# A transformer-like block on one core: the first four tiles of x are only centred, and their scale is applied to two products

## The chip, the core and the metric

The kernel runs on one core of a Trainium2 chip. A core has five instruction streams that run side by side and wait for each other by semaphores: PE (TensorE, matrix products, with PEld for the loading of weights), DVE (VectorE), ACT (ScalarE), POOL (GpSimd) and SP (SyncE, which here only starts DMA transfers). DMA transfers can be started by SP and by ACT. The metric is the device time of one execution in microseconds (us); what is compared is the median over several executions.

## What is computed

`x` has 2048 rows of 448 values (bf16). It is normalised by rows, `xn = (x - mean) / sqrt(var + eps)`, and `xn` feeds two branches; the output is `x + A(xn) + B(xn)`.

```python
def _A_ref(x, wqkv, w_phi, wo):                 # linear attention, 16 heads of 28
    q, k, v = split(x @ wqkv)
    pq, pk = q @ w_phi, k @ w_phi               # by head
    phi_q = concat(softmax(pq), softmax(-pq)); phi_k = concat(softmax(pk), softmax(-pk))
    kv = einsum("bhsf,bhsd->bhfd", phi_k, v); z = phi_k summed over s
    num = phi_q @ kv; den = phi_q @ z + 1e-6
    return (num / den) @ wo

def _B_ref(x, w1, w2, w3, w4):
    h = gelu(layernorm(x) @ w1)
    hs = (four column groups of h, shifted by 1, -1, 2, -2 rows) @ w2
    x1 = x + hs
    return x1 + gelu(layernorm(x1) @ w3) @ w4

xn = layernorm(x)
return x + _A_ref(xn, ...) + _B_ref(xn, ...)
```

## The kernel before, in words

The 2048 rows are 16 tiles of 128 rows. Every tile goes through the same steps, and each engine's stream is written out by hand: the order of the calls in the source is the order on each engine, and a recording layer adds the semaphore waits. There is no planner. Nearly every instruction is issued from a helper, so the profile shows few lines: L188 is a matrix product, L192 a transpose on PE, L196 an ACT activation, L200 any elementwise operation (on DVE or POOL), L203 a transposing DMA and L206 a plain DMA.

**The head.** SP and ACT start the loads of x (`xtok`), of V's weights (`wv`, in two halves, one from each engine) and of W1 (`w1`, the same). For each tile DVE takes row statistics (`ln_stats`: one BATCH_NORM_STATS2 on `xtok`, one BATCH_NORM_AGGREGATE that writes mean and variance to `mv`). POOL makes the scale from the variance (`ln1_scale`: an addition and a power, written to `rs`), and DVE subtracts the mean and multiplies with the scale in one TENSOR_SCALAR (`ln1_apply`), which writes `xn`. PE transposes the tile by four 128x128 products with an identity (`xn_T`), ACT copies the result to `xnT`, and PE multiplies it with `wv` and `w1`. V's products leave PSUM as a copy into `vaug` (by ACT or DVE), W1's through a GELU on ACT into `h_tok`, whose scale `rs[..., 4]` is that of the second layer norm. `octet(g)` does this for four tiles: pairs of V and W1 products in eight PSUM banks, full 128-row products first, 64-row tails after. In octet 0 the transposes of tiles 0 to 3 stand among the first products, those of 4 and 5 after the V products of tiles 2 and 3; the transposes of tiles 6 and 7 open octet 1, in banks 4 and 5, which hold the V products of tiles 2 and 3 until DVE has copied them out. Before the first real product PE runs idle products on a constant (`spin`). Tiles 12 to 15 are transposed by DMA (`xn_Td`).

**The middle.** SP transposes `h_tok` to `hT` by DMA (`h_T`), which the shifted products with `w2` read (`w2_tile`, row tile i needs `hT` of tile i+1 too); their sum with `xn` is x1 (`w2_add`), which takes the place of `xn`. K and Q products of four tiles at a time (`ks`, `qs`) go through two exponentials on ACT; DVE and POOL normalise K (`k_norm`); `kv_tile` sums over all 16 tiles in banks 4 and 5. `g_T` transposes the normalised x1 to `gT` by DMA (two buffers, one for each group of four tiles), `eq_T` the exponentials of Q to `eqT`.

**The last stage.** A list `plan` gives for each of nine stages the bank pairs of W3 products (`chunks`, 14 for each group of four row tiles) and the steps between them: `N` (num_tile) a Q product with kv and its division on DVE and POOL, `O` (o_T) a DMA transpose of the result, `E` (eq_T) the next two transposes of Q, `Ff` (fin_full) the products with `w4` and `wo` that need `O`'s transpose, `St` the store, `W`, `ga` and `sc` what is left of the middle.

The places that the change touches are the list of first loads, `ln1_some` and `octet(0)` in the head, the order of `ks`, `qs`, `k_norm` and `w2_tile` in the middle (K's tiles in the order 0, 4, 8, 12, Q's first four behind K's 4 to 7), and two rows of `plan`.

Of the kernel before, what the change touches and what calls it, by code (L numbers as in the profile page):

```python
# [11 lines left out]
LN_EPS = 1e-5  # L12
# [196 lines left out]
def bass_parallel_sum__linear_kernel_hedgehog__mixer_s_mlp__prompt_kernel(  # L209
# [15 lines left out]
    with es:  # L225
# [35 lines left out]
        gT = new("gT", 2 * KC * 512).rearrange("p (b c s) -> p b c s", b=2, c=KC)  # L261
        eq_r = region("eq", 8 * 2 * 512 * 2)
# [29 lines left out]
        mv2 = new("mv2", NT * 8, F32).rearrange("p (t c) -> p t c", t=NT)  # L292
        rs2 = new("rs2", NT * 8, F32).rearrange("p (t c) -> p t c", t=NT)
# [90 lines left out]
        busy = gT[:, 0, 0, 0:256]  # L384
        R.ew(dve, "memset", busy, 1.0)
# [61 lines left out]

        def ln1_apply(eng, i):
            ln_apply(eng, halves(xn[:, i, :]), lap(xtok[:, i, :]), mv, rs, i, 2)
# [3 lines left out]
        def spin(n, cols):  # L453
            for _ in range(n):
                R.mm(banks[3][:, 0:cols], busy[:, 0:128], busy[:, 0:cols], True, True)
# [11 lines left out]
        def xn_T(i, b):  # L467
            b = banks[b]
            for kc in range(KC):
                R.tr(tview(b)[:, 128 * kc:128 * kc + 128], xn[:, i, 128 * kc:128 * kc + 128], ident[:, :])  # L470
            R.act(xnT[:, :, 128 * i:128 * i + 128], tview(b).rearrange("p (c d) -> p c d", c=KC), ACT.Copy)

        def xn_Td(i):
            R.dma_t(xnT[:, :, 128 * i:128 * i + 128], xn[:, i, :])
# [19 lines left out]
        def v_pair(i, b):  # L494
            def out(eng="ACT"):
                vd = vaug[:, i:i + 2, :].rearrange("p t (h e) -> p t h e", e=HP)[:, :, :, 0:DH]
                vs = two(b)[:, :, 0:D].rearrange("p t (h e) -> p t h e", e=DH)
                if eng == "ACT":
# [5 lines left out]
        def w_pair(i, b):  # L504
            def out(ks=(0, 1)):
                for k in ks:
                    R.act(h_tok[i + k].rearrange("p (m d) -> p m d", m=NM)[:, :, 0:CR],
                          banks[b + k][:, 0:D].rearrange("p (m d) -> p m d", m=NM), ACT.Gelu_apprx_tanh,
                          scale=rs[:, i + k, 4:5])
            return [tok(w1, i, b), tok(w1, i + 1, b + 1)], out  # L510

        def k_pair(i, b):
            def out():
                for s in range(2):
                    R.act(phik[:, i:i + 2, s, :], two(b)[:, :, 0:D], ACT.Exp, scale=1.0 - 2.0 * s)
# [41 lines left out]
        def k_norm(i, eng=pool):  # L557
            for j in (i, i + 1):
                ph = phik[:, j, :, :].rearrange("p s (h e) -> p (s h) e", e=DH)
# [6 lines left out]
        def kv_tile(i):  # L566
            for c in range(NC):
                b = banks[4 + c // 2][:, 224 * (c % 2):224 * (c % 2) + 224].rearrange("p (s f) -> p s f", s=2)
                for j in range(2):
                    R.mm(b[64 * j:64 * j + 64, :, 56 * j:56 * j + 56],  # L570
                         vaug[:, i, 128 * c + 64 * j:128 * c + 64 * j + 64],
                         phik[:, i, :, CR * c + 56 * j:CR * c + 56 * j + 56],
                         i == 0 and c % 2 == 0, i == NT - 1)
# [30 lines left out]
        def w2_add(i, b, stats=True):  # L604
            b = banks[b]
            x1, x = xn[:, i, 0:D], xn[:, i, :]
            x = bass.AP(x.tensor, x.offset, [list(x.ap[0]), [288, 2], [1, 224]])
# [337 lines left out]
```

## Time and profile before

| | before |
|---|---|
| median of 3 runs | 181.69 us (181.62 to 182.08) |
| the profiled execution's own time | 181.43 us |
| its span (first to last instruction) | 179.7 us |
| granted TensorE clock in the rows | 1.000 |
| PE busy | 175.9 us, 98% of the span |
| DVE, POOL, ACT busy | 117.6, 94.6, 80.2 us |
| moved by DMA | 21.04 MB, 117 GB/s |

A timeline row reads: start, length, engine, line, operation, output and input tiles, shapes, how many instructions were merged into the row, and in brackets the idle time of the engine ahead of it with what ended it. PE's rows overlap, since products are pipelined: a row's length holds the drain of the last product. The rows of DMA issues (SPq, ACTq) show how long the issuing engine was occupied; when the data landed stands in the table of DMA issues.

### The profile page before, as it was taken

Reading aid. Unit: us, or ns where it says so; the run is one execution under the profiler, and the core shown is the slowest. Engines: PE = TensorE matmul, PEld = TensorE weight load, DVE = VectorE, ACT = ScalarE, POOL = GpSimd, SP = SyncE. Lnnn points to the kernel's source line nnn. Section 1 sums busy time; section 2 is a strip of 40 time slices with the busy share of each in tenths; the row PEclk is TensorE's granted clock in tenths of the full one; section 3 lists DMA queues with packets and bytes.
Section 4 is the critical chain, followed back from the end, with each engine's and each line's share of the span. In section 5 each row is a group of like instructions: output and inputs, shape, how many; then the busy total and the mean of one; then the engine's idle time right before and its main releaser. Section 6 shows DMA issues by size and latency. Waiting matters only on the chain.

```text
span 179.7 us, 3181 instructions
## 1 busy us (share of the span) xinstructions
PE 175.9 (98%) x1218; PEld 90.5 (50%) x1218; DVE 117.6 (65%) x269; ACT 80.2 (45%) x99; POOL 94.6 (53%) x144
## 2 busy tenths in 40 slices
PE   7999999999999999999999999999999999999994
PEld 5554655454445444654554654553554544635564
DVE  5898679659999999584594296196282352655531
ACT  2378881798999639777105104103206006014000
POOL 7774582067999797002457526037835063151660
PEclk9999999999999999999999999999999999999999
DMA  5998555499465498473245545432554654120231
GB/s 166 338 218 134 102 87 104 89 341 223 89 90 106 98 277 172 91 160 60 58 88 89 89 101 104 110 62 58 113 112 99 82 138 96 43 59 28 55 106 51
DMA packets 59142, 21.04 MB, mean 117 GB/s; under 512 B 50744, under 2 KB 58616, under 8 KB 59128
## 3 DMA queue, kind: packets, MB, share of 16 engines
q1 hardware_dynamic: 55656, 16.56, 45.8%
q10 hardware_dynamic: 3472, 4.29, 8.0%
q8 instruction: 9, 0.15, 0.3%
q14 instruction: 5, 0.04, 0.1%
HBM read 7.08 MB, written 1.84 MB: 50 GB/s over the span
## 4 chain that ended last, share of the span: by engine, by line
PE 95%; DVE 3%; ACT 0%; issue 0%
PE bank L188 93%; PE bank L192 2%; DVE vaug L200 1%; DVE st L200 1%; DVE xn L200 1%; ACT xnT L196 0%; DVE mv L200 0%; DVE gT L200 0%
## 5 line engine op out<-in xcount | busy, mean ns | idle before, releaser
L196 ACT ACTIVATE phik<-bank 128x1024 bf16<-128x1024 f32 (+1 forms) x44 | 40.2, 991 | 68.1 <-PE bank L188 67.9
L188 PE MATMUL bank<-gT,w 128*128 128x512 bf16 (+1 forms) x224 | 46.1, 380 | 0.1
L188 PE MATMUL bank<-w,phik 128*128 128x448 bf16 (+2 forms) x238 | 45.2, 342 | 0.0
L200 DVE TENSOR_TENSOR vaug<-bank,vaug 128x464 f32<-128x464 f32 (+3 forms) x65 | 33.1, 514 | 17.4 <-PE bank L188 12.3
L200 POOL TENSOR_TENSOR xnT<-vaug 128x196 bf16<-128x196 f32 (+1 forms) x32 | 18.0, 585 | 49.2 <-DVE vaug L200 49.2
L188 PEld LDWEIGHTS bank<-w,phik 128*128 128x128 bf16 x238 | 22.6, 98 | 18.4 <-issue 0.2
L188 PEld LDWEIGHTS bank<-gT,w 128*128 128x128 bf16 (+1 forms) x224 | 17.9, 97 | 24.0 <-issue 5.1
L200 POOL TENSOR_TENSOR phik<-phik,rks 128x896 bf16<-128x896 bf16 x15 | 25.8, 1754 | 1.0 <-DVE rks L200 0.9
L200 POOL TENSOR_TENSOR vaug<-xn,xtok 128x448 f32<-128x448 bf16 x16 | 16.3, 1029 | 1.4 <-DVE vaug L200 1.4
L200 DVE TENSOR_TENSOR xn<-bank,xn 128x448 bf16<-128x448 f32 x16 | 9.4, 597 | 11.5 <-PE bank L188 11.5
L200 DVE TENSOR_REDUCE ksum<-phik 128x32 f32<-128x896 bf16 x16 | 16.6, 1035 | 0.0
L200 DVE RECIPROCAL vaug<-bank 128x16 f32<-128x16 f32 x16 | 3.6, 228 | 17.9 <-PE bank L188 17.9
L188 PE MATMUL bank<-wo,xnT 128*128 128x448 bf16 (+3 forms) x68 | 14.7, 344 | 0.0
L200 POOL TENSOR_TENSOR rs<-mv,mhalf 128x2 f32<-128x2 f32 (+1 forms) x16 | 13.8, 863 | 1.3
L188 PE MATMUL bank<-w,hT 112*128 112x448 bf16 x64 | 14.2, 352 | 0.0
L188 PE MATMUL bank<-wv,xnT 128*128 128x448 bf16 (+1 forms) x64 | 14.0, 354 | 0.1
L188 PE MATMUL bank<-w,xnT 128*128 128x448 bf16 (+1 forms) x64 | 13.9, 352 | 0.0
L188 PE MATMUL bank<-wpk,xnT 128*128 128x448 bf16 (+1 forms) x64 | 12.2, 354 | 0.0
L188 PE MATMUL bank<-wpq,xnT 128*128 128x448 bf16 (+1 forms) x64 | 12.1, 354 | 0.0
L196 ACT ACTIVATE eq<-bank 128x896 bf16<-128x896 f32 x12 | 10.0, 923 | 1.4 <-PE bank L188 1.4
L200 POOL TENSOR_SCALAR mv<-mv 128x4 f32<-128x4 f32 x4 | 0.8, 203 | 18.2 <-DVE mv L200 18.2
L200 DVE BATCH_NORM_STATS2 st<-xtok 128x6 f32<-128x448 bf16 x16 | 9.8, 612 | 0.8 <-DMA xtok<-in_A_x_dram 0.7
(66 smaller groups left out, 179.2 us busy)
## 6 DMA issues: line engine op xcount, KB each, us to landing
w<-in_B_w_dram ACTq DMA_DIRECT2D x2, 896.0 KB, 6.4
out_dram<-vaug SPq DMA_DIRECT2D x15, 112.0 KB, 1.9
w<-in_B_w_dram ACTq DMA_DIRECT2D x1, 1568.0 KB, 8.7
xtok<-in_A_x_dram SPq DMA_DIRECT2D x2, 448.0 KB, 6.8
wo<-in_A_wo_dram SPq DMA_DIRECT2D x2, 224.0 KB, 2.8
w<-in_B_w_dram SPq DMA_DIRECT2D x1, 392.0 KB, 4.4
hi<-eq SPq DMA_TRANSPOSE x24, 2.5
xtok<-in_A_x_dram SPq DMA_DIRECT2D x3, 112.0 KB, 3.0
```

The lines of the kernel that those rows point to most:

```text
L188: self.op("PE", lambda e: e.matmul(out, lhsT, rhs, start=start, stop=stop, skip_group_check=True), [out], [lhsT, rhs])
L192: self.op("PE", lambda e: e.transpose(out, in_, ident), [out], [in_, ident])
L196: self.op("ACT", lambda e: e.activation(out, in_, func, **kw), [out], [in_] + aps)
L200: self.op(eng, lambda e: getattr(e, name)(out, *args, **kw), [out], aps)
```

## The change

Tiles 0 to 3 of x are no longer scaled before the transposes. `ln1_center` on DVE subtracts the mean and multiplies with 1.0, right behind the tile's own statistics, into `xc`, which lies in the second buffer of `gT`. PE transposes `xc`. The scale is applied later: to V's products as they leave PSUM (one instruction for each of two tiles, with the scale `rs[..., 2]`, where one copy took both tiles), and to W1's products in the GELU's scale, for which `ln1_first` makes `rw` in three small DVE operations. K, Q and the residual still need the scaled tiles, so POOL makes them later (one TENSOR_SCALAR for four means, four `ln1_apply` into `xc`), and four more DMA transposes on SP write them over the first four tiles of `xnT`. K's order is turned so that tiles 0 to 3 come last (4, 8, 12, 0; `phik`'s slots and `kv_tile`'s sum too), and Q's first four tiles move behind K's 12 to 15.

With it: x's first tile is loaded in two halves of 64 rows, one from SP and one from ACT; both halves of `wv` are started ahead of x's tile 2, x's tile 5 goes to SP; the constant of the idle products is set by POOL as its first instruction, and the idle products are 31 of 128 columns, then 4; the copy of tile 0's transposes is made in two halves; the transposes of tile 5 stand three products later; W1's tiles 0 and 1 leave PSUM together; and in two stages of the plan `O` stands ahead of `E`.

```diff
+        xc = gT[:, 1, :, :]
...
+        rw = new("rw", 4 * 8, F32).rearrange("p (t c) -> p t c", t=4)
...
-        load_x(0, 1)
+        busy = gT[:, 0, 0, 0:128]
+        R.ew("POOL", "memset", busy, 1.0)
+        for k, e in enumerate(("SP", "ACT")):
+            R.dma(xtok[64 * k:64 * k + 64, 0, :], x2d[64 * k:64 * k + 64, :], e)
         load_x(1, 1, "ACT")
+        load_lap(wv, A_wqkv[:, 896:1344], ("ACT", "SP"))
         load_x(2, 1)
-        load_lap(wv, A_wqkv[:, 896:1344], ("ACT", "SP"))
         load_x(3, 1, "ACT")
+        load_lap(w1, B_w1, ("ACT", "SP"))
         load_x(4, 1)
-        load_lap(w1, B_w1, ("ACT", "SP"))
-        load_x(5, 1, "ACT")
+        load_x(5, 1)
...
+        def ln1_first():
+            R.ew(dve, "scalar_tensor_tensor", rw[:, :, 0], rs[:, 0:4, 3], (1.0 + LN_EPS) ** -0.5, mv[:, 0:4, 2],
+                 op0=ALU.mult, op1=ALU.mult)
+            for k in range(2):
+                R.ew(dve, "tensor_tensor", rw[:, :, 1 + k], rw[:, :, k], rs[:, 0:4, 2], op=ALU.mult)
...
+        def ln1_center(i):
+            R.ew(dve, "tensor_scalar", halves(xc[:, i, :]), lap(xtok[:, i, :]), mv[:, i, 0:1], 1.0, op0=ALU.subtract,
+                 op1=ALU.mult)
...
+            for c in (slice(0, 4, 3), slice(1, 3)) if i < 1 else (slice(0, 4),):
+                R.act(xnT[:, c, 128 * i:128 * i + 128], tview(b).rearrange("p (c d) -> p c d", c=KC)[:, c, :], ACT.Copy)
...
+                if i < 4:
+                    for k in range(2):
+                        s = rs[:, i + k, 2:3]
+                        if eng == "ACT":
+                            R.act(vd[:, k, :, :], vs[:, k, :, :], ACT.Copy, scale=s)
+                        else:
+                            R.ew(eng, "tensor_scalar", vd[:, k, :, :], vs[:, k, :, :], s, 1.0, op0=ALU.mult, op1=ALU.mult)
...
-                          scale=rs[:, i + k, 4:5])
+                          scale=rs[:, i + k, 4:5] if i > 3 else rw[:, i + k, 2:3])
...
-        def ln1_some(a, n):
-            for i in range(a, a + n):
-                ln1_stats(i, 1, 0)
-                if i:
-                    ln1_apply(dve, i - 1)
-                if i == 4:
-                    ln1_again(0, 4)
+        def ln1_some():
+            for i in range(4):
+                ln_stats(st, mv, xtok, i)
+                ln1_center(i)
+                if i % 2:
+                    ln1_scale(i - 1, 2, 0)
+            ln1_stats(4, 1, 0)
+            ln1_stats(5, 1, 0)
+            ln_stats(st, mv, xtok, 6)
+            ln1_apply(dve, 4)
+            ln_stats(st, mv, xtok, 7)
+            ln1_scale(6, 2, 0)
+            ln1_apply(dve, 5)
+            ln1_first()
...
-                spin(19, 256)
-                xn_T(0, 4)
-                spin(5, 128)
-                xn_T(1, 5)
+                spin(31)
+                xn_T(0, 4, xc)
+                spin(4)
+                xn_T(1, 5, xc)
...
+        R.ew(pool, "tensor_scalar", rs[:, 0:4, 1], mv[:, 0:4, 0], -1.0, 0.0, op0=ALU.mult, op1=ALU.add)
+        for i in range(4):
+            ln1_apply(pool, i)
...
+        h_T(5)
+        for i in range(4):
+            xn_Td(i)
+        for i in range(6, 8):
...
-        ks(0)
+        ks(4)
...
-        batch([nxt(k_pair, 4)], [nxt(k_pair, 6)], folds)
+        batch([nxt(k_pair, 8)], [nxt(k_pair, 10)], folds)
...
-            (0, 2, 6, [(Ff, 6), (St, 4), (N, 8, 0), (E, 12), (O, 8), (N, 9, 6), (E, 13), (O, 9), (Ff, 7), (St, 5),]),
+            (0, 2, 6, [(Ff, 6), (St, 4), (N, 8, 0), (O, 8), (E, 12), (N, 9, 6), (O, 9), (E, 13), (Ff, 7), (St, 5),]),
```

What stands in a row now, at the places where instructions move. First DVE at the start of the program, from its first statistics on (`st` and `mv` hold them, `xtok` is x as loaded, `rs` the scale). Before:

```order
L200 BN_STATS st<-xtok 128x6
L200 BN_AGGR mv<-st 128x2
L200 BN_STATS st<-xtok 128x6
L200 BN_AGGR mv<-st 128x2
L200 TENSOR_SCALAR xn<-xtok,mv,rs 128x512
```

After:

```order
L200 BN_STATS st<-xtok 128x6
L200 BN_AGGR mv<-st 128x2
L200 TENSOR_SCALAR gT<-xtok,mv 128x512
L200 BN_STATS st<-xtok 128x6
L200 BN_AGGR mv<-st 128x2
```

The first tile is centred directly behind its own statistics, and the operation reads no `rs`, so POOL is no longer between them.

DVE again, up to the V products of tiles 2 and 3 that it takes out of banks 4 and 5. Before:

```order
L200 BN_STATS st<-xtok 128x6
L200 BN_AGGR mv<-st 128x2
L200 TENSOR_SCALAR xn<-xtok,mv,rs 128x512
L200 CAST vaug<-bank 128x32x28
L200 BN_STATS st<-xtok 128x6
```

After:

```order
L200 TENSOR_SCALAR xn<-xtok,mv,rs 128x512
L200 SCALAR_TENSOR_TENSOR rw<-rs,mv 128x4
L200 TENSOR_TENSOR rw<-rw,rs 128x4 x2
L200 BN_STATS st<-xtok 128x6
L200 BN_AGGR mv<-st 128x2
L200 TENSOR_SCALAR xn<-xtok,mv,rs 128x512 x2
L200 TENSOR_SCALAR vaug<-bank,rs 128x16x28 x2
```

One copy of both tiles became two scaled ones, and the last two tiles of x stand directly ahead of them.

SP's first loads. Before:

```order
L206 DMA xtok<-in_A_x_dram 128x448 x2
L206 DMA wv<-in_A_wqkv_dram 128x2x448
L206 DMA xtok<-in_A_x_dram 128x448
L206 DMA w<-in_B_w_dram 128x2x448
L206 DMA xtok<-in_A_x_dram 128x2x448
```

After:

```order
L206 DMA xtok<-in_A_x_dram 64x448
L206 DMA wv<-in_A_wqkv_dram 128x2x448
L206 DMA xtok<-in_A_x_dram 128x448
L206 DMA w<-in_B_w_dram 128x2x448
L206 DMA xtok<-in_A_x_dram 128x448 x2
L206 DMA xtok<-in_A_x_dram 128x2x448
```

x's tile 2 was SP's second load and is its third, behind a half of `wv`.

SP's transposes in the middle (`hT` from three tiles of `h_tok`, called hi, w and h here; `hi<-eq` are those of Q). Before:

```order
L203 DMA_TRANSPOSE xnT<-xn 128x4x128 x4
L203 DMA_TRANSPOSE hi<-in_A_wqkv_dram 128x448 x2
L203 DMA_TRANSPOSE hT<-hi 128x4x128 x3
L203 DMA_TRANSPOSE hT<-w 128x4x128 x3
L203 DMA_TRANSPOSE gT<-g_tok 128x4x128 x4
L203 DMA_TRANSPOSE hi<-eq 128x4x128 x8
```

After:

```order
L203 DMA_TRANSPOSE xnT<-xn 128x4x128 x4
L203 DMA_TRANSPOSE hi<-in_A_wqkv_dram 128x448 x2
L203 DMA_TRANSPOSE hT<-hi 128x4x128
L203 DMA_TRANSPOSE xnT<-gT 128x4x128 x4
L203 DMA_TRANSPOSE hT<-hi 128x4x128 x2
L203 DMA_TRANSPOSE hT<-w 128x4x128 x3
L203 DMA_TRANSPOSE gT<-g_tok 128x4x128 x4
L203 DMA_TRANSPOSE hT<-w 128x4x128
L203 DMA_TRANSPOSE hi<-eq 128x4x128 x8
```

Four transposes are new, and all that stands behind them on SP moves back by four places, the second group of `gT` too.

More of the change, by code (lines that the diff above doesn't have):

```diff
@@ L514, in out @@
                 for s in range(2):
-                    R.act(phik[:, i:i + 2, s, :], two(b)[:, :, 0:D], ACT.Exp, scale=1.0 - 2.0 * s)
+                    R.act(phik[:, (i + 12) % 16:(i + 12) % 16 + 2, s, :], two(b)[:, :, 0:D], ACT.Exp, scale=1.0 - 2.0 * s)
             return [tok(wpk, i, b), tok(wpk, i + 1, b + 1)], out
@@ L571, in kv_tile @@
                          vaug[:, i, 128 * c + 64 * j:128 * c + 64 * j + 64],
[L572 to L573 removed]
+                         phik[:, (i + 12) % 16, :, CR * c + 56 * j:CR * c + 56 * j + 56],
+                         i == 4 and c % 2 == 0, i == 3)
         def kv_copy():
@@ L744, in octet @@
                 xn_T(i + 4, 0)
-                xn_T(i + 5, 1)
+                if g:
+                    xn_T(i + 5, 1)
             if late:
                 late()
-            w[1]((1,))
+            w[1]((1,) if g else (0, 1))
             v2[1](evac)
-            for o in w2[0]:
+            for k, o in enumerate(w2[0]):
                 full(o, False)
+                if not g and not k:
+                    xn_T(5, 1)
             w2[1]()
-        ln1_some(0, 8)
+        ln1_some()
         ln_stats(st, mv, xtok, 8)
-        ln1_apply(dve, 7)
+        for i in range(6, 8):
+            ln1_apply(dve, i)
         octet(0, "DVE")
@@ L776, in bass_parallel_sum__linear_kernel_hedgehog__mixer_s_mlp__prompt_kernel @@
             load_wT(0, c)
-        for i in range(5, 8):
+        h_T(5)
+        for i in range(4):
+            xn_Td(i)
+        for i in range(6, 8):
             h_T(i)
```

65 lines of the change are left out of this document (33 added, 32 removed).

## The prediction

> **What bounds the kernel now.** I read the busy times first, then the chain that ended last, then the timeline of the first 16 us.
>
> ```profile
> PE 175.9 (98%) x1218; PEld 90.5 (50%) x1218; DVE 117.6 (65%) x269; ACT 80.2 (45%) x99; POOL 94.6 (53%) x144
> ```
>
> ```profile
> 1.26 4.24 PE bank L188 x19
> ...
> 21.79 54.50 PE bank L188 x430
> ```
>
> The chain is PE nearly throughout, and in the 54.50 us of 430 products nothing but PE stands. So a change pays only where PE idles or runs idle products: ahead of the first real transposes at 5.46, between them, and in single stalls. The work behind the head cannot get shorter; it can only start earlier or be held up anew.
>
> ```profile
> 3.07 0.59 DVE L200 BATCH_NORM_STATS2 st<-xtok 128x6 f32<-128x448 bf16 x1 [0.75 <-DMA xtok<-in_A_x_dram]
> ...
> 4.99 0.41 DVE L200 TENSOR_SCALAR xn<-xtok,mv,rs 128x512 bf16<-128x512 bf16 x1 [0.38 <-POOL rs L200]
> ...
> 5.46 0.61 PE L192 MATMUL bank<-ident,xn 128*128 128x128 bf16 x4
> ...
> 6.46 0.63 DVE L200 BATCH_NORM_STATS2 st<-xtok 128x6 f32<-128x448 bf16 x1
> ...
> 8.30 0.39 PE L192 MATMUL bank<-ident,xn 128*128 128x128 bf16 x4
> ...
> 8.53 0.73 PE L188 MATMUL bank<-w,xnT 128*128 128x448 bf16 x3
> ...
> 10.03 0.62 DVE L200 BATCH_NORM_STATS2 st<-xtok 128x6 f32<-128x448 bf16 x1
> 10.69 0.18 DVE L200 BATCH_NORM_AGGREGATE mv<-st 128x2 f32<-128x6 f32 x1
> 10.98 0.41 DVE L200 TENSOR_SCALAR xn<-xtok,mv,rs 128x512 bf16<-128x512 bf16 x1
> 11.31 0.62 DVE L200 BATCH_NORM_STATS2 st<-xtok 128x6 f32<-128x448 bf16 x1
> ...
> 12.06 0.38 DVE L200 TENSOR_SCALAR xn<-xtok,mv,rs 128x512 bf16<-128x512 bf16 x1
> ...
> 13.63 1.08 DVE L200 CAST vaug<-bank 128x896 bf16<-128x896 f32 x1
> ...
> 14.77 0.45 PEld L192 LDWEIGHTS bank<-ident,xn 128*128 128x128 bf16 x8 [0.34 <-DVE vaug L200]
> ...
> 15.23 0.73 PE L188 MATMUL bank<-wv,xnT 128*128 128x448 bf16 x3
> ```
>
> DVE works nearly without a break from 3.07 to 14.71. The last place in the head where PE waits for it is the eight transposes of tiles 6 and 7, which need banks 4 and 5 copied out; behind them PE goes on at 15.23. I call this the gate: whatever moves the gate moves the end.
>
> **The change part by part.** The pace at the gate has two possible owners, DVE and the loads.
>
> *DVE.* Before, from tile 3's statistics (6.46) to the copy's end (14.71) are 8.25 us. A tile's TENSOR_SCALAR starts 0.75 behind the statistics ahead of it (11.31 to 12.06), or 0.95 where it waits for POOL (10.03 to 10.98). After, the stretch holds one TENSOR_SCALAR fewer (the centring is done behind the own statistics): -0.33, the step from 10.98 to the next operation at 11.31. Waits for POOL go: two of 0.2 and one of 0.1 at tile 2, -0.48. One small operation more than before: +0.20. Centring waits for its own aggregate, start at 0.87 (10.03 to 10.69, 0.18 and 0.03) instead of 0.75: +0.12. The copy becomes two:
>
> ```profile
> 27.29 1.14 DVE L200 CAST wpk<-bank 128x448 bf16<-128x448 f32 x2
> ```
>
> Wait-free, two copies of this size take 1.14 against 1.08: +0.06 (between 0 and 0.15). Sum 8.25 - 0.33 - 0.48 + 0.20 + 0.12 + 0.06 = 7.82. Ahead of it stands tile 2's statistics and centring, 1.18 (0.87 and 0.31). With 0.06 to start, and 0.28 from the copy's end through the second tile's transposes, PE passes the gate at L + 9.34, if DVE's tile 2 starts at L, the landing of x's tile 2. It passed at 15.23, so L = 5.89 breaks even. Without any wait for loads DVE starts tile 2 at about 5.1 (first statistics some 0.3 sooner for the halved load, an estimate, at 2.75; two tiles of 1.18).
>
> *The loads.* Landing is issue time and the time in the table of DMA issues.
>
> ```profile
> xtok<-in_A_x_dram SPq DMA_DIRECT2D x3, 112.0 KB, 3.0
> xtok<-in_A_x_dram ACTq DMA_DIRECT2D x3, 112.0 KB, 4.7
> wv<-in_A_wqkv_dram ACTq DMA_DIRECT2D x1, 224.0 KB, 4.1
> wv<-in_A_wqkv_dram SPq DMA_DIRECT2D x1, 224.0 KB, 5.2
> w<-in_B_w_dram ACTq DMA_DIRECT2D x1, 224.0 KB, 5.4
> ```
>
> ```profile
> 1.26 0.46 ACTq L206 DMA_DIRECT2D wv<-in_A_wqkv_dram  x1
> 1.72 0.43 SPq L206 DMA_DIRECT2D wv<-in_A_wqkv_dram  x1
> 1.75 0.49 ACTq L206 DMA_DIRECT2D xtok<-in_A_x_dram  x1
> 2.27 0.46 ACTq L206 DMA_DIRECT2D w<-in_B_w_dram  x1
> ```
>
> So `wv`'s ACT half landed at 5.4 as the queue's 336th KB, x's tile 3 at 6.45 and `wv`'s SP half at 6.9 (both 448), W1's ACT half at 7.7 (672). Tile 2 moves from SP's second place (started beside `wv`'s ACT half at about 1.26, landed 3.0 later, 4.3) to the third, with 392 KB on its queue. Its bounds are 4.3 and 6.9; the middle of the two ACT rows is 5.9, and a tile of x lands 0.45 sooner than a weight half with as many bytes (6.45 against 6.9). I take L = 5.45: the gate at 14.79, 0.44 sooner. W1's ACT half moves to 728 KB, at the slope of the last two rows (1.25 us for 224 KB) 8.0. From W1's first product to the gate PE needs 15.23 - 8.53 - 0.06 (its stall there) = 6.64: 14.70, so DVE decides. The idle products take 0.223 each for 256 columns (4.24 / 19); 31 of half that from about 1.1 on end at 4.5, so real transposes start there, 1.0 sooner. The halved first load, the sooner idle products and the halved copy gain nothing of their own, since the loads cover them; leaving POOL out starts the first TENSOR_SCALAR 1.05 sooner (3.07 + 0.87 against 4.99), and of that 0.44 reaches the gate.
>
> The Trainium skill (DMA: Bandwidth & Descriptors, "Issuing engines are not separate DMA queues") says that transfers from all issuing engines run on the same 16 DMA engines and interleave. By that, halving saves only issue time, and tile 2 lands with all the bytes ahead on both queues, at the unshifted middle of 5.9; the sum would have nothing at the gate instead of 0.44. The rows of equal bytes with different landings say it is not bytes alone.
>
> *SP and POOL.* Four transposes more:
>
> ```profile
> 24.45 5.13 SPq L203 DMA_TRANSPOSE xnT<-xn  x4
> ...
> 37.28 5.52 SPq L203 DMA_TRANSPOSE hT<-w  x3
> ...
> 71.14 5.13 SPq L203 DMA_TRANSPOSE gT<-g_tok  x4
> ```
>
> ```profile
> SPq L203 <- DVE g_tok L200: 5.9, 1, 5.9
> ```
>
> ```profile
> 78.51 5.78 PE L188 MATMUL bank<-gT,w 128*128 128x512 bf16 x29
> ```
>
> They cost 5.1 on SP, which is busy from 24 to 66 us, so everything behind them comes 5.1 later, until SP's wait of 5.9 for DVE ahead of `gT`'s second group takes it up. During a large weight load a transpose holds SP for 1.84 (5.52 / 3) instead of 1.28; two to four more fall into that, 1.1 to 2.2. So the group starts 0.3 to 1.4 later (5.1 + 1.1 - 5.9, and so on). Its last transpose, issued at 75.0, landed at 77.5 (the landing time is in the next rows), and now by 78.9. PE needs it six products into 78.51, at 79.8. Between 0 and 0.3 (one more transpose held for 1.3); I take 0. K's 12 to 15 now stand ahead of tile 5's W2 product, which so starts behind one batch of 2.9 from 42.6 on, at 45.5, and needs at its second product (45.7) the transpose of `h_tok`'s tile 6. That one takes the place of the third in the row at 37.28 (issued at 40.0):
>
> ```profile
> gT<-g_tok SPq DMA_TRANSPOSE x16, 2.5
> ...
> hT<-w SPq DMA_TRANSPOSE x4, 5.6
> ```
>
> ```profile
> 42.61 3.02 PE L188 MATMUL bank<-wpq,xnT 128*128 128x448 bf16 x16
> ```
>
> It lands (second row; the first is for the group above) at 45.6: between 0 and 0.3, taken as 0. POOL's four new TENSOR_SCALARs take 0.41 on DVE (10.98); even at three times that, an estimate of 5 us, they fit POOL's longest idle stretch, which follows them:
>
> ```profile
> 37.13 0.20 POOL L200 TENSOR_SCALAR mv<-mv 128x4 f32<-128x4 f32 x1 [9.10 <-DVE mv L200]
> ```
>
> They cost nothing; without that cover they would delay K's normalisation by those 5. The turned order of K and Q keeps counts and the turns of the banks:
>
> ```profile
> 54.35 3.35 ACT L196 ACTIVATE phik<-bank 128x896 bf16<-128x896 f32 x4 [0.28 <-PE bank L188]
> ```
>
> ACT waited for PE here, so it is not behind. Its last four exponentials now follow a batch with no W2 tile behind it and end up to 0.75 later against the first W3 products; between 0 and 0.7, taken as 0, since the first bank pair is free one pair of exponentials sooner.
>
> *O ahead of E.*
>
> ```profile
> 133.97 2.50 SPq L203 DMA_TRANSPOSE hi<-eq  x2
> 136.52 1.26 SPq L203 DMA_TRANSPOSE xnT<-xnT  x1
> ...
> 140.84 0.30 PEld L188 LDWEIGHTS bank<-wo,xnT 128*128 128x128 bf16 x3 [0.39 <-DMA xnT<-xnT]
> ```
>
> In one of the two stages PE waits for this transpose; of the 0.39 a weight load hides 0.27, leaving 0.12. Issued 2.5 sooner it is there: -0.12. The other stage has no such stall.
>
> **Sum.** -0.44 - 0.12 = -0.56 against the profiled execution's 181.43 (span 179.7 and 1.73 around it): 180.9. The median of the runs lies 0.26 above it; the forecast for the median is 181.1.
>
> **Rivals.**
> (a) Loads are no bound: tile 2 by 5.1 and W1 by 7.6 at the latest. The gate at 14.4, 0.85 sooner, with 0.12: 180.7. For it: before, x's tile 2 landed well ahead of its use. Against: landings up to 5.4 us behind the issue.
> (b) Nothing comes of the centring, because tile 2 waits for all bytes ahead (L = 5.9): only -0.12 remains, 181.6. For it: the two ACT rows with 336 and 448 KB. [...]
> (c) Slower: SP's third load lands like SP's third load before, `wv`'s half, at 6.9. The gate at 16.3, 1.05 later; less 0.12: 182.6. It decides from L = 6.6 on. For it: same queue, same place, similar bytes. Against: half its size.
> (d) The second group of `gT` lands 1.7 later than I reckon, for transposes held longer by W4's load: a stall of 0.8 at 79.8, 181.9.
> The Trainium skill (TensorE: Matmul & The Clock Gate, "What's actually happening") has the array at half rate until a free-running window of about 3.4 us was busy; the trace agrees that early transposes take longer (0.61 at 5.46, 0.39 at 8.30). If the window fell one turn later, real products to 10 us would run at half rate, an estimate of 1 us; I give it 0.02, within slower.
>
> **How the numbers follow.** The bound of same is 0.3%, 0.55 us, about what a measurement here can tell from no change. Forecast 0.40 (180.8 to 181.4, two thirds of it over the bound), (a) 0.18, (b) 0.17, (c) 0.16, (d) and late clock 0.09. Faster 0.27 + 0.18 = 0.45; same 0.13 + 0.15 = 0.28; slower 0.27. The forecast's own range is 180.8 to 181.4; the range to hold 8 in 10 reaches from beyond (a), 180.4, into (c), 182.3.
>
> **What would show it.** Right: DVE's first TENSOR_SCALAR at 3.7 to 4.0 with no wait for POOL, real transposes at 4.5, the gate passed near 14.8, no stall at `gT`'s second group and none at `wo`'s products in the stage at 140. Wrong: a wait of DVE for `xtok` at tile 2 that reaches past 5.9, PE idle ahead of W1's first product past 8.5, or a new PE wait for a DMA near 45 or 80.

## The result, and the profile after

The changed kernel takes 182.86 us (median of six, 182.73 to 183.21), the kernel before 181.78 us in the same comparison (181.59 to 182.08): a ratio of 1.006, 95% interval 1.0046 to 1.0074. The forecast was 181.1 (180.8 to 181.4; the range to hold 8 in 10 ended at 182.3); the change costs 1.08 us, and the measured time lies beyond both. The profiled execution took 182.73 us with a span of 181.0, against 181.43 and 179.7: 1.30 more.

The first line of the changed kernel's page gives the busy times; the rows below it are from its chain of waits (start, length, what).

```profile
PE 174.0 (96%) x1220; PEld 90.4 (50%) x1229; DVE 117.1 (65%) x270; ACT 80.7 (45%) x101; POOL 96.0 (53%) x144
```

```profile
0.82 0.57 ACTq L206
1.42 0.85 ACTq L206
2.31 0.46 ACTq L206
2.79 4.55 DMA xtok<-in_A_x_dram
7.37 0.64 DVE st L200
...
10.22 0.71 POOL rs L200
10.96 0.41 DVE xn L200
...
28.95 4.16 DMA xnT<-xn
33.11 0.14 issue
33.25 25.57 PE bank L188 x179
```

Before, the chain was PE nearly throughout. Now it runs through three issues on ACT and the landing of x's tile 3 into DVE's list (DVE waited for it only 0.04), and past the gate once more through a DMA: a transpose of one of tiles 12 to 15, 4.16 us long. The head as the timeline shows it (DVE's rows, then PE's):

```profile
3.39 0.63 DVE L200 BATCH_NORM_STATS2 st<-xtok 128x6 f32<-128x448 bf16 x1 [0.23 <-DMA xtok<-in_A_x_dram]
...
4.27 0.35 DVE L200 TENSOR_SCALAR gT<-xtok,mv 128x512 bf16<-128x512 bf16 x1
4.96 0.63 DVE L200 BATCH_NORM_STATS2 st<-xtok 128x6 f32<-128x448 bf16 x1 [0.33 <-DMA xtok<-in_A_x_dram]
...
6.10 0.62 DVE L200 BATCH_NORM_STATS2 st<-xtok 128x6 f32<-128x448 bf16 x1
...
7.37 0.63 DVE L200 BATCH_NORM_STATS2 st<-xtok 128x6 f32<-128x448 bf16 x1
...
10.63 0.18 DVE L200 BATCH_NORM_AGGREGATE mv<-st 128x2 f32<-128x6 f32 x1
10.96 0.41 DVE L200 TENSOR_SCALAR xn<-xtok,mv,rs 128x512 bf16<-128x512 bf16 x1
...
14.26 1.27 DVE L200 TENSOR_SCALAR vaug<-bank,rs 128x448 bf16<-128x448 f32 x2
```

```profile
4.68 0.40 PE L192 MATMUL bank<-ident,gT 128*128 128x128 bf16 x4 [0.36 <-DVE gT L200]
...
6.24 0.40 PE L192 MATMUL bank<-ident,gT 128*128 128x128 bf16 x4 [0.94 <-DVE gT L200]
...
8.90 0.74 PE L188 MATMUL bank<-w,xnT 128*128 128x448 bf16 x3 [0.61 <-DMA w<-in_B_w_dram]
...
15.09 0.89 PE L192 MATMUL bank<-ident,xn 128*128 128x128 bf16 x8
15.82 0.73 PE L188 MATMUL bank<-wv,xnT 128*128 128x448 bf16 x3
```

Centring does start sooner (4.27 against 4.99), and so do the real transposes (4.68 against 5.46). But DVE waits for tile 1 until 4.96; tile 2, landed at 5.11, follows without a break only at 6.10, and tile 3 at 7.37. Before, tiles 1 and 2 were taken up at these times, and tile 3 at 6.46:

```profile
3.79 0.60 DVE L200 BATCH_NORM_STATS2 st<-xtok 128x6 f32<-128x448 bf16 x1
...
5.32 0.62 DVE L200 BATCH_NORM_STATS2 st<-xtok 128x6 f32<-128x448 bf16 x1
```

Tile 1 had landed at 3.18 before and lands at 4.93 now; tile 3 at 6.43 and now at 7.35. W1's first product waits until 8.90 (8.53 before), and the gate is passed at 15.82, not 15.23.

The second loss stands at 32.4. PE's timeline there, and the table of DMA between 29.8 and 31.0 (of the issues in it the one that PE waits for, with its time to landing):

```profile
32.41 0.35 PE L188 MATMUL bank<-wv,xnT 64*128 64x448 bf16 x1
33.25 0.35 PE L188 MATMUL bank<-wv,xnT 64*128 64x448 bf16 x1 [0.49 <-DMA xnT<-xn]
```

```profile
q8 instruction: 1, 0.02, 7.9%
issues: line engine op xcount, KB each, median us to landing
xnT<-xn SPq DMA_TRANSPOSE x1, 4.2
```

The transpose issued at 28.95 landed 4.2 us later, at 33.1; its like before took 2.5 (28.31 to 30.83, one microsecond ahead of its use). While it was under way one packet of 16 KB of the kind "instruction" came through queue q8, at 30.15. Before, that packet came at 31.92, behind the landing.

The starts of PE's products, compared stage by stage, give the whole difference: +0.59 at the gate, +0.83 between the gate and K's first product (the wait at 32.4), 0.00 from there to 140, -0.13 at 140. Sum +1.29 of the 1.30. Rival (d)'s stall didn't happen in this execution: the last transpose of `gT`'s second group landed at 79.90 (77.50 before). The first product that needs it is the seventh of its row, as before at 79.8; with PE 1.42 later it stands at about 81.2, so 1.3 us were to spare (2.3 before), less than the packet at 32 cost its transpose. Another packet of q8 came at 79.91, just behind the landing.

### The profile page after: what moved, and what is told of

Read it like the earlier page. It is cut to its first block, busy times and chain, and to the rows that moved or that the text cites. A ratio compares the mean times of both kernels' runs of the same rounds, so it can differ in the third digit from the quotient of the medians.

```text
span 181.0 us, 3211 instructions
## 1 busy us (share of the span) xinstructions
PE 174.0 (96%) x1220; PEld 90.4 (50%) x1229; DVE 117.1 (65%) x270; ACT 80.7 (45%) x101; POOL 96.0 (53%) x144
## 4 chain that ended last, share of the span: by engine, by line
PE 73%; DVE 12%; DMA 5%; POOL 4%; issue 2%; ACT 2%; ACTq 1%
PE bank L188 73%; DVE st L200 4%; DVE vaug L200 3%; POOL rs L200 3%; DMA xtok<-in_A_x_dram 3%; DVE xn L200 2%; DMA xnT<-xn 2%; ACT phik L196 2%; DVE mv L200 1%; ACTq L206 1%; POOL mv L200 1%; DVE wpk L200 1%; POOL xn L200 0%; DVE rs L200 0%; PE bank L192 0%
## 5 line engine op out<-in xcount | busy, mean ns | idle before, releaser
L188 PE MATMUL bank<-gT,w 128*128 128x512 bf16 (+1 forms) x215 | 44.1, 379 | 0.9 <-DVE vaug L200 0.3
L200 DVE TENSOR_TENSOR vaug<-bank,vaug 128x464 f32<-128x464 f32 (+3 forms) x65 | 33.1, 514 | 17.4 <-PE bank L188 13.5
L200 DVE TENSOR_TENSOR xn<-bank,xn 128x448 bf16<-128x448 f32 x12 | 7.1, 590 | 10.7 <-PE bank L188 10.7
L200 POOL TENSOR_TENSOR rs<-mv,mhalf 128x4 f32<-128x4 f32 (+1 forms) x13 | 12.7, 974 | 1.0
L200 DVE BATCH_NORM_STATS2 st<-xn 128x6 f32<-128x448 bf16 x16 | 9.9, 619 | 0.4
```

The source lines that it names most:

```text
L188: self.op("PE", lambda e: e.matmul(out, lhsT, rhs, start=start, stop=stop, skip_group_check=True), [out], [lhsT, rhs])
L200: self.op(eng, lambda e: getattr(e, name)(out, *args, **kw), [out], aps)
```

## Experiments

For every run its gate and its later waits were read in the same way from its profiled execution. The kernel before, run beside each set, had medians of 181.78 to 181.80. In all fourteen profiles that one's time is 166.2 us behind its gate, plus its later waits, less 0.13 where the wait at 140 is missing, to within 0.15 us. Several kernels spread by up to 2.65 us over their executions (one by more, as said there); where the text names a wait it is that of the profiled one.

**What moves the wait at 32.** If q8's packet does it, its place should follow PE's count of products, of which eleven idle ones more stand ahead. The first kernel takes the changed kernel back to 24 idle products, with narrower products to fill the time:

```diff
-                spin(31)
+                spin(20, 192)
...
-                spin(4)
+                spin(4, 128)
```

> The changed kernel with 24 idle products, as before, in place of 35 (20 of 192 columns and 4 of 128 in place of 31 and 4 of 128; the time they cover stays within 0.2 us). Theory (instruction fetch): the 0.83 us that PE waits at 32.4 for the transposes of tiles 12 to 15 comes from a 16 KB packet of the instruction queue q8, which came at 31.92 in the kernel before and at 30.15 now, because it follows PE's count of instructions and eleven idle products more stand ahead of it. With 24 the packet comes at about 32 to 32.6 again, behind the transposes' landing, and the stall goes: 182.86 - 0.83 = 182.0 (181.9 to 182.2), with the gate still near 15.8. Rival (SP late): the stall comes from SP, whose transposes start 0.65 later, and from the four more transposes; the count of idle products then changes nothing: 182.9 (182.7 to 183.0).

Measured: 183.59 us (181.79 to 184.44), ratio 1.0072 (1.004 to 1.0105). The packet came at 32.57, the fourth transpose landed in 2.5 us, and the wait at 32 was gone; the three quickest executions (181.79, 181.96, 181.99) are at the forecast of 182.0. The profiled one took 183.86, for two other reasons:

```profile
6.59 2.45 PE L188 MATMUL bank<-wv,xnT 128*128 128x448 bf16 x6
...
9.26 1.22 PE L188 MATMUL bank<-w,xnT 128*128 128x448 bf16 x3
```

Six V products took 2.45 us where they take 1.59 in the changed kernel, three of W1 1.22 against 0.74: PE ran at half pace until 10, and the gate came at 16.38. This is the late clock that the prediction gave 0.02. The Trainium skill (TensorE: Matmul & The Clock Gate, "What's actually happening") has the window of the gate free-running, so that the same kernel can turn fast at different places. The same idle products with the old loads, below, were followed by full pace from 5.78 on (four transposes in 0.40, here 0.61 at 6.19); that agrees, but PE had no pause of 0.50 there as it has here ahead of 6.19, and no run shows the window itself. The other loss, 1.38 at 80.7, is rival (d), with a q8 packet at 79.83.

The next kernel takes the idle products of the kernel before (19 of 256 columns and 5 of 128), which keep PE busy longer:

```diff
-                spin(31)
+                spin(19, 256)
...
-                spin(4)
+                spin(5, 128)
```

> The changed kernel with the idle products of the kernel before (19 of 256 columns and 5 of 128), all else as changed. The first run with 24 idle products lost the wait near 32 but had two new losses in its profiled execution: products at half pace up to 10.0, and a wait of 1.38 at 80.7 for the last transpose of gT's second group, which a q8 packet at 79.8 held up. Theory (three separate places): the longer idle products keep the pace, so the gate is near 15.8; the q8 packet comes at about 32 and the wait near 32 is gone: 182.0 in executions in which gT's second group lands in time, up to 1.4 more in those in which a packet meets it; median 182.0 to 182.8. Rival (SP late): the wait near 32 is back, 182.8 to 183.0 in all executions.

Measured: 182.26 us (181.71 to 184.16), ratio 1.004 (1.0007 to 1.0073); six of twelve executions lie between 181.71 and 182.07. Full pace from the first V product, packet at 32.80, no wait at 32. The profiled execution (184.11) is one of the late ones. Its PE row behind 80, and the DMA between 79.0 and 80.4:

```profile
82.60 0.59 PE L188 MATMUL bank<-gT,w 128*128 128x512 bf16 x2 [1.78 <-DMA gT<-g_tok]
```

```profile
q8 instruction: 1, 0.02, 5.9%
issues: line engine op xcount, KB each, median us to landing
gT<-g_tok SPq DMA_TRANSPOSE x1, 3.6
```

The third transpose of the group, issued at 77.51, landed only at 81.92, the fourth at 82.40; a loss of 1.94. Not all of it is this packet's: the fourth was issued at 78.81, so that at the usual 2.5 it would have landed at 81.3, and PE needed it at 80.7. So the changed kernel has two places at which a q8 packet can meet a transpose with little slack, 32 and 80: the three profiles with 35 idle products lost at 32, and of the three with 24 and all of the change's transposes two lost at 80.

The other direction, 50 idle products:

```diff
-                spin(31)
+                spin(46, 88)
```

> The changed kernel with 50 idle products in place of 35 (46 of 88 columns and 4 of 128, which take about the same time). Theory (instruction packet): the second packet of q8 moves another fifteen products forward, from 30.15 to 27 to 28.5, and meets the second or third of the four transposes instead of the fourth; that one lands up to 1.7 later, at 31 to 31.9, still ahead of the 32.4 at which PE needs it, so the wait near 32 goes or falls below 0.3: 182.0 to 182.3, unless a later packet meets gT's second group (1.4 to 1.9 more). Rival: the wait does not hang on the packet's place: 182.8 to 183.0.

Measured: 182.53 us (181.94 to 183.59), ratio 1.0035 (1.0016 to 1.0054); four executions between 181.94 and 182.04, the profiled one among them; what the others lost is not shown. The packet came at 28.27 and met the second transpose, which landed 4.7 us behind its issue where its like before took 2.5; PE waited 0.23 ahead of its product at 30.73 and not at 32. The changed kernel's wait therefore hangs on the packet's place.

Last, the kernel before with 35 idle products, in the same time:

```diff
-                spin(19, 256)
+                spin(30, 160)
```

> The kernel before with 35 idle products in place of 24 (30 of 160 columns and 5 of 128 in place of 19 of 256 and 5 of 128; their time stays 4.2 us), nothing else. Theory (instruction fetch): the packet of q8 comes some eleven products sooner, at about 29.8 to 30.2 in place of 31.92, while the transposes of tiles 12 to 15 are in flight (issued 24.45 to 28.31, last landing 30.83, needed at 31.8), and the first one at about 14.4 in place of 16.42: a wait of 0.4 to 0.9 near 32, 182.2 to 182.7. Rival (SP late): without SP's later start nothing is lost, since there was 1.0 us of slack: 181.8 (181.6 to 181.9).

Measured: 182.06 us (181.48 to 182.86), ratio 1.0012 (0.9995 to 1.003): nothing decided. The packet moved less than expected, to 31.61, and the last transpose had landed at 31.36, 0.25 us ahead of it. In all fourteen traces this packet came when PE had begun 208 to 218 products (the next one at 328 to 336); that scatter of ten products is nearly 2 us, so eleven idle products more make a meeting likely, not sure.

**What moves the gate.** The changed kernel with the first loads of the kernel before, then the same with 24 idle products as above:

```diff
-        for k, e in enumerate(("SP", "ACT")):
-            R.dma(xtok[64 * k:64 * k + 64, 0, :], x2d[64 * k:64 * k + 64, :], e)
+        load_x(0, 1)
         load_x(1, 1, "ACT")
+        load_x(2, 1)
         load_lap(wv, A_wqkv[:, 896:1344], ("ACT", "SP"))
-        load_x(2, 1)
...
```

> The changed kernel with the first loads of the kernel before (x's first tile whole, the old order and the old engines), all else as changed. Theory (loads): the gate at 15.82 is late because x's tile 3 lands at 7.35 and W1's second half at 8.86, against 6.43 and 8.24 before. With the old loads DVE starts tile 3 at about 6.6 and ends the copy 8.16 later (as measured now), at 14.8, W1's first product starts at 8.3 to 8.5 and PE passes the gate at 15.0 to 15.2: 0.6 to 0.8 sooner. The wait near 32 stays: 182.1 to 182.3. Rival (DVE): the gate is late because centring, two small copies and the three operations for rw make DVE's list longer, whatever lands when: gate at 15.6 to 15.8, 182.7 to 182.9.

> Both edits at once: old loads and 24 idle products in the changed kernel. If both theories hold and the two losses are separate, 182.86 - 0.83 - 0.7 = 181.3 (181.1 to 181.6), which is faster than the kernel before by 0.4: the centring's own gain (gate 15.0 to 15.2 against 15.23) and 0.1 for the order of o and q. If the loads are no cause, 182.0; if the idle products are none, 182.1; if neither, 182.9.

Measured: 182.86 us (182.56 to 183.61), ratio 1.0064 (1.0043 to 1.0084), and 182.12 us (181.14 to 183.64), ratio 1.0032 (1.0001 to 1.0064). In the first, tile 3 landed at 7.22 even with the old loads, the gate came at 15.69, and the wait at 32 took 1.08: in time it was no better than the changed kernel, against the expectation. DVE's list there was no longer than in the changed kernel (8.16) and DVE stood idle for tile 3 for 0.47, so a load was late again, though issued at 1.75 as in the kernel before. The five profiles with the old loads have tile 1 landing at 3.18 to 3.50 and tile 3 at 6.18 to 7.22; the six with the new ones 4.75 to 5.07 and 7.02 to 7.44. Tile 1 is late in each of them, tile 3 by 0.6 in the mean. In the second's profiled execution (181.29) tile 3 landed at 6.67, the gate came at 15.22, and no later wait stood anywhere. Its four quickest executions (181.14 to 181.29) lie below the quickest of the kernel before beside it (181.40); the slowest take 2.5 us more.

The reverse tells more: the kernel before with the new loads alone, that is with the same lines the other way round.

> The kernel before with the changed kernel's first loads alone (x's first tile in halves from SP and ACT, wv ahead of x's tile 2, tile 5 on SP). Theory (loads): x's tile 3 lands at about 7.3 and W1's last half at 8.6 to 8.9, in place of 6.4 to 6.9 and 8.2; the gate, which stood 8.8 behind tile 3's landing in the two profiles of the old kernel, comes at 15.9 to 16.2 in place of 15.2 to 15.7: 182.2 to 182.6 against 181.8. Rival (DVE): the gate is late for the centring's own operations and the loads have slack: 181.7 to 181.9.

Measured: 182.76 us (182.09 to 183.63, and one execution of twelve at 186.28), ratio 1.005 (1.0028 to 1.0072). In the median the loads alone cost about what the whole change costs. The profiled execution (182.09), one of the two quickest, has the gate at 16.03, 0.80 later, and no other loss; what the slower ones lost in addition is not shown. DVE's rows for tiles 1 and 3:

```profile
4.84 0.63 DVE L200 BATCH_NORM_STATS2 st<-xtok 128x6 f32<-128x448 bf16 x1 [0.64 <-DMA xtok<-in_A_x_dram]
...
7.18 0.62 DVE L200 BATCH_NORM_STATS2 st<-xtok 128x6 f32<-128x448 bf16 x1
```

DVE waits 0.64 for tile 1 and not at all for tile 3, which comes later only because tile 1 did.

Which part of the loads? The changed kernel with tile 0 whole on SP, all else as changed:

```diff
-        for k, e in enumerate(("SP", "ACT")):
-            R.dma(xtok[64 * k:64 * k + 64, 0, :], x2d[64 * k:64 * k + 64, :], e)
+        load_x(0, 1)
```

> The changed kernel with x's first tile loaded whole by SP; the order of the other loads stays as changed (wv ahead of tile 2, tile 5 on SP). Theory (a place in ACT's list): the half tile on ACT pushes tile 1, wv, tile 3 and W1 one place back; without it tile 1 lands at 3.2 to 3.6 in place of 4.9, tile 3 at 6.4 to 7.2 in place of 7.35, W1's ACT half at 7.7 to 8.4 in place of 8.86; the gate comes at 15.1 to 15.7 in place of 15.82 and the wait near 32 stays: 182.2 to 182.7. Rival (the order): what delays tile 3 and W1 is wv's halves ahead of them, not the half tile; the gate stays at 15.8: 182.8 to 183.0.

Measured: 182.58 us (182.20 to 184.24), ratio 1.0042 (1.002 to 1.0064), gate at 15.47, tile 1 landed at 3.57, tile 3 at 6.15, W1's ACT half at 7.51; the wait at 32 stayed (1.03, packet at 30.49). So tiles 1 and 3 and W1 were late for the half tile, not for the order: it takes a place in ACT's list, and issuing is slower with it. Of the 0.59 at the gate 0.24 is left: here DVE began at 3.40 (3.07 before) and waited 0.12 for tile 2, which stands behind `wv` and landed at 5.87, so the order may have a part in that. ACT's rows of issues in the changed kernel, and in this one:

```profile
0.82 1.46 ACTq L206 DMA_DIRECT2D xtok<-in_A_x_dram  x2
2.31 0.46 ACTq L206 DMA_DIRECT2D wv<-in_A_wqkv_dram  x1
2.79 0.49 ACTq L206 DMA_DIRECT2D xtok<-in_A_x_dram  x1
3.31 0.46 ACTq L206 DMA_DIRECT2D w<-in_B_w_dram  x1
```

```profile
0.82 0.41 ACTq L206 DMA_DIRECT2D xtok<-in_A_x_dram  x1
1.25 0.46 ACTq L206 DMA_DIRECT2D wv<-in_A_wqkv_dram  x1
1.74 0.52 ACTq L206 DMA_DIRECT2D xtok<-in_A_x_dram  x1
2.28 0.46 ACTq L206 DMA_DIRECT2D w<-in_B_w_dram  x1
```

Tile 1, the second in the row of two, is issued 0.60 us later (at 1.42), and everything behind it 1.03 to 1.06. The change before and after: tile 1 was issued at 0.82 and landed 2.36 later, now at 1.42 and landed 3.51 later; tile 3 1.75 and 4.68, now 2.79 and 4.55; W1's half 2.27 and 5.45, now 3.31 and 5.55.

**Without SP's four transposes.** K and Q of tiles 0 to 3 can use the centred tiles, if the exponentials take the row's scale (K's lines; Q's are alike; the idle products are those of the kernel before):

```diff
+                        for k in range(2):
+                            R.act(phik[:, (i + 12) % 16 + k, s, :], banks[b + k][:, 0:D], ACT.Exp,
+                                  scale=rs[:, i + k, 2 + 3 * s:3 + 3 * s])
...
-        for i in range(4):
-            xn_Td(i)
```

> As the last, and the four transposes that SP issues more are left out: K and Q of tiles 0 to 3 are computed from the centred tiles that xnT already holds, and the exponentials take the row's scale (or its negative, one small POOL operation more), one tile at a time. Theory: the spread of 2.6 us with 24 idle products came from SP, whose gT second group landed at 79.9 to 82.2 against a need of about 79.9; without the four transposes (5.1 to 6 us on SP) it lands by 78 and no packet can cost anything there: 182.0 with a spread below 1.0. ACT has eight exponentials more, of half the size, beside PE's products: no cost. Rival (ACT or pace): the spread stays above 1.5 us, because it comes from the pace of the first products, or the exponentials hold up the banks: 182.3 to 183.5.

Measured: 182.96 us (182.68 to 183.27), ratio 1.0054 (1.0033 to 1.0076). The spread fell from 2.45 (twelve executions) to 0.59 us (eight) and `gT`'s second group landed at 78.07, in place of 82.40: those transposes were what exposed it. But the exponentials were not free, as the rival had it:

```profile
48.45 4.30 ACT L196 ACTIVATE eq<-bank,rs 128x448 bf16<-128x448 f32 x8 [0.27 <-PE bank L188]
52.59 4.36 ACT L196 ACTIVATE phik<-bank,rs 128x448 bf16<-128x448 f32 x8
```

```profile
58.62 3.62 PE L188 MATMUL bank<-gT,w 128*128 128x512 bf16 x16 [0.62 <-ACT eq L196]
```

Eight halves take 4.3 us where four took 3.35, and a batch leaves ACT only some 0.28 of idle time; PE lost 1.01 at W3's first products.

**Tile 3 ahead of `wv`.** The same kernel with the first loads of the kernel before, and in them x's first four tiles first (shown against that list):

```diff
         load_x(0, 1)
         load_x(1, 1, "ACT")
         load_x(2, 1)
+        load_x(3, 1, "ACT")
         load_lap(wv, A_wqkv[:, 896:1344], ("ACT", "SP"))
-        load_x(3, 1, "ACT")
```

> The changed kernel with the old idle products, without the four transposes, and with x's first four tiles loaded whole and all ahead of wv (SP, ACT, SP, ACT), then wv, tile 4, W1, tile 5. Theory (loads): tile 3 lands at 5.0 to 5.9, so DVE never waits: tile 3's statistics at 6.6 to 6.8, the copy's end 8.16 later, the gate at 15.0 to 15.2; wv lands at 6.4 to 7.0, in time for V's products or 0.3 late, which the gate doesn't see. With 0.12 for the order of o and q: 181.3 to 181.5, steadier than the kernel before. Rival (wv): V's products start later than 7.0, PE rather than DVE sets the gate, 15.4 to 15.8: 181.7 to 182.0.

Measured: 182.52 us (182.35 to 183.25), ratio 1.0035 (1.0019 to 1.0051); 1.01 of it is the exponentials' again, which the expectation had not counted. Tile 3 landed at 4.18, DVE never waited for it (statistics at 6.84), and the copy ended 8.14 later, at 14.98; the gate came at 15.27. That is 11.87 behind DVE's first statistics (3.40, tile 0 landed late here), as in the run with old loads and 24 idle products (3.35 to 15.22); in the kernel before it is 12.16 (3.07 to 15.23), and 12.17 (3.31 to 15.48) in its run with `O` ahead of `E` alone, below. So with no load in its way the centring, with the small edits of the head beside it, is worth 0.29 us.

So the same order of loads was put into the kernel before, with `O` ahead of `E` and without centring; and `O` ahead of `E` alone.

> The kernel before with x's first four tiles loaded ahead of wv and with o ahead of q, without centring. Theory (no gain in centring): DVE's list from tile 3's statistics to the copy's end is 8.25 long without and 8.14 with centring, so with tile 3 no longer late the old list passes the gate as soon as the new one: at 8.8 behind tile 3's statistics, 15.2 to 15.6, in all executions: 181.3 to 181.7, less spread than the kernel before (181.45 to 182.83). Rival (wv): V's products wait for wv and PE sets the gate, 15.6 to 16.0: 181.8 to 182.1.

> The kernel before with o ahead of q in the two stages, nothing else. Theory: of the wait of 0.12 that PE has at 140.5 for o's transpose nothing is left, and no other wait comes: 181.79 - 0.12 = 181.7 (181.5 to 181.8). Rival: q's transposes, now 1.3 to 2.5 later, are late for the next num_tile: 181.8 to 182.2.

Measured: 181.53 us (181.47 to 182.19), ratio 0.9982 (0.9968 to 0.9996), faster than both kernels; and 181.60 us (181.54 to 182.52), ratio 0.9995 (0.998 to 1.001), no change to be seen. The first is not faster by a sooner gate: it stood at 15.51 in the profiled execution, with no wait of PE for DVE, because V's products waited for `wv` until 7.53, as its rival said. Eleven of its twelve executions lie within 181.47 to 181.68, while the kernel before's 35 beside it reach from 181.53 to 182.69; which of its two edits narrows them is not shown.

## Why the prediction was wrong, by its own steps

**The sum.** It had -0.44 at the gate, -0.12 at 140 and nothing else; measured were +0.59, -0.13 and +0.83.

**The gate: tile 1 was not priced.** L, the landing of tile 2, was 5.11, sooner than the 5.45 taken, and rivals (b) and (c) varied this landing alone. But L + 9.34 lets DVE take tile 2 up when it lands, and that supposes that tile 1 is done by then (at about 5.1, without any wait for loads). Tile 1 had moved behind the half tile on ACT and landed at 4.93, not 3.18; DVE was free for tile 2 only at 6.10, 0.65 behind the forecast's 5.45. Tile 3, which landed at 7.35 and was not priced either, made it 0.74 (7.37 against 6.63); with tile 1 in time it would have held DVE up to the same 7.37. In all six profiles with the new loads DVE waits for tile 1 (0.06 to 0.64), in three of them for tile 3 as well. The rows to see it with were quoted: ACT's issues. One issue more at the head of ACT's list moves the whole list: tile 1 was issued 0.60 later, and its landing took 1.15 longer, for which no run shows the reason; W1's ACT half was reckoned by KB on the queue (8.0) and landed at 8.86, where its issue was 1.04 later. The rule of the Trainium skill (DMA: Bandwidth & Descriptors, "Issuing engines are not separate DMA queues"), that only issue time is saved and that it is usually small, led to the same oversight: here issue time was lost, 0.60 to 1.04 for each of these loads. Landing by all bytes ahead, as the prediction read it, would have put tile 2 at 5.9; it landed at 5.11.

**The halved first tile** was taken to bring the first statistics to 2.75, and to cost nothing. They came at 3.39, since the halves landed at 3.02 and 3.30, where whole tiles landed at 3.01 to 3.38; and the half cost ACT's list the 0.60 to 1.04 us.

**DVE's ledger** gave 7.82 from tile 3's statistics to the copy's end; it is 8.16, and 8.14 in the run with no load waits. Two terms: the two scaled copies take 1.27, not the 1.14 of two plain ones (0.13), and of the 0.48 of POOL waits 0.23 came back, at 10.63 to 10.96, where tile 4's scale stands behind that of tiles 2 and 3 on POOL (the chain's row at 10.22). The 0.74 and the 0.34 make 1.08; less the 0.06 that the formula has for DVE's start, they are the 1.03 by which the gate came later than forecast (15.82 against 14.79), to 0.01. With no load in its way the new head is 0.29 shorter from the first statistics to the gate; the prediction's own figures for that case (2.75 to about 14.44 against 3.07 to 15.23) make it 0.47. The loads took more than that away.

**The idle products, not in the sum.** The change has eleven more of them, and the prediction gave them no effect but to pass time. The wait of 0.83 near 32 hangs on them: a q8 packet met a transpose of tiles 12 to 15, and with 24 or 50 idle products this wait is gone.

**SP's four transposes, taken as 0.** They cost nothing in the changed kernel's profile, but took slack: the group was reckoned to land by 78.9 with 0.9 to spare, and landed at 79.90 with 1.3, since PE itself was 1.42 late. A packet costs more than that. Rival (d) happened where one came, for that and not for W4's load, and took 1.38 to 1.94 (forecast 0.8). The transpose of `h_tok` at 45 cost nothing in the changed kernel and 0.17 in one run. The turned order of K and Q and POOL's four operations cost nothing, as taken: between K's first product and 140 the two kernels keep the same distance.

**`O` ahead of `E`, -0.12.** The number came in the profile, but what the edit removes is no standing wait, so this was luck. The wait at 140.84 in the quoted profile was the trace of one q8 packet; DMA between 136.4 and 136.6, and between 138 and 139, in the kernel before:

```profile
xnT<-xnT SPq DMA_TRANSPOSE x1, 4.3
```

```profile
q8 instruction: 1, 0.02, 6.9%
```

That transpose needed 4.3 us instead of 2.5, since a packet came at 138.46. The wait is missing as well from both profiles with the old order in those stages (35 idle products; new loads, where a packet met the transpose too and it landed just in time), and the edit alone made no difference that its twelve executions could show.

**What was missing.** No step asked what else uses the DMA engines while a transpose is under way, nor what the idle products do besides passing time. Of the 632 DMA transposes issued behind 84 us in the fourteen traces, 571 had no q8 packet begin between issue and landing; they landed in 2.48 us (median). In 27 cases a packet began 1.0 to 2.35 us behind the issue: 4.16 (3.61 to 4.94). In 29 it began in the first microsecond: 3.24. In 5 it began in the last 0.15 us: 2.48, no effect.

**The centre and the others.** Rival (c), slower through a late load, was the nearest: right in direction and kind, but on the wrong queue. That its time (182.6) came near is luck: the gate with the -0.13 makes 182.2 of it (181.78 + 0.59 - 0.13), and the rest is the wait near 32, which no rival had. (a) and (b) fell. "Wrong" was to be seen in PE idle ahead of W1's first product past 8.5, and was: 8.90.

## What to carry to other kernels

An edit that splits a load, or puts one more ahead, moves every later issue of that engine's list: price each load behind it by its new issue time, and follow every tile that the bounding engine takes up in turn, not just the one that the edit names: here the one ahead of it was late. A transfer with less slack than one packet of another queue costs (1.7 us here) will be late in some executions, and a wait that a single profile shows may be such a meeting: look for it in a second profile before counting its removal as a gain. Idle instructions are not free of side effects: here they moved the place at which a packet of another queue came.

## What the runs showed of the hardware that was not expected

- One packet of 16 KB of kind "instruction" on q8, 0.9 to 1.7 us long, holds up a DMA transpose by about 1.7 us (4.16 against 2.48) if it begins 1.0 to 2.35 us behind the issue. It comes nine or ten times in an execution, the second time when PE has begun 208 to 218 products, the third at 328 to 336, in every trace; that it brings PE's instructions is argued from these counts, not shown.
- Issuing 64 rows took longer than issuing 128: 0.57 to 0.58 us on SP and ACT against 0.39 to 0.42, and ACT's next issue took 0.85 against 0.46. The Trainium skill (Perfetto Trace Analysis, "DMA Instruction — HWDGE (DVE, Sync)") has an issue's row hold a wait for a descriptor generator that engines share; whether that is the longer time here no run shows.
- An ACT activation of 448 columns a row with a scale from memory took 0.54 us (4.30 for eight), one of 896 columns 0.84: the two halves with their scales cost 0.95 us more for each batch of four tiles. How much of it is the scale, no run shows.
